# Batch 1 of a fused attention and feed-forward kernel: A@V in one burst behind FFN2, squares and a T copy on ScalarE, the first q cast by two engines

## The chip, the cores and the metric

The kernel runs on one core of a Trainium2 chip. A core has five engines with a queue each: TensorE (PE in the profile; its weight loads are PEld), VectorE (DVE), ScalarE (ACT), GpSimd (POOL) and SyncE (SP). Each works through its own queue in order, and they wait for one another through semaphores. The metric is the device time of one execution in microseconds.

## The reference

For 8 batches, 12 heads, 448 positions and a head dimension of 64, attention without softmax, and then a feed-forward layer with a PReLU:

```python
scores = scale * np.matmul(q, k.transpose(0, 1, 3, 2))      # scale = 1/sqrt(64)
attn = np.maximum(scores, 0.0) ** 2 / S                     # S = 448
attn_out = np.matmul(attn, v)
x = attn_out.transpose(0, 2, 1, 3).reshape(B * S, H * D)    # 3584 x 768
h = x @ w_in                                                # 768 x 2048
g = np.maximum(h, 0.0) + alpha * np.minimum(h, 0.0)
out = g @ w_out                                             # 2048 x 768
```

## The kernel before

**Quads and chunks.** Four heads of one batch make a quad; there are 3 quads a batch and 24 in all, numbered through. Positions are cut into 7 chunks (`j`) of 64. For a chunk, `score_mm` (L170) issues four matmuls of 64x64 weights and 448 columns, which run side by side in the four quarters of TensorE's array, into a pair of PSUM banks. `relu` (L181) moves the result to SBUF as bf16, on ScalarE ("A") or VectorE ("D"), and `square` (L189) squares it, on VectorE unless told otherwise. `sc` issues scores and relus and puts the chunks on the list `late`; `sq(k)` squares the first k of the list. `attnv` (L197) multiplies a quad's seven squared chunks by v (28 matmuls, accumulated in one pair of banks) and writes its halves to `xT`, one by ScalarE and one by VectorE.

**T.** Scores want q and k with the head dimension on the partitions. For the first quads `turn_pe` (L142) transposes on TensorE, 14 small matmuls for q and 14 for k, each set into one PSUM bank (or into more, by `cuts`), and copies the bank to `T` with VectorE or ScalarE. From quad 6 on `turn_dma` (L158) has VectorE rearrange and a DMA transpose.

**Feed-forward.** FFN1 unit `ff` of batch `b` (`f1`, L251) is six matmuls of 448 columns into one bank (`f1_mm`), and then `f1_out`: ScalarE computes neg = relu(-h), VectorE computes gT = neg * beta + h (L247, which frees the bank), and one chunk of `late` is squared, on VectorE. FFN2 (`f2`, L256) takes 128 positions and half of the output columns: 16 matmuls of 384 columns over all 16 units' gT, a copy by ScalarE, and two stores by SyncE. Two batches share a `gT`.

**Order.** No planner is at work: each engine's queue is the order in which the Python code issues, written out by hand for batches 0 and 1 (L277 to L377) and looped after that. PSUM's eight banks are handed out by `take_pair` and `take_bank`, the longest unused first, so an order on TensorE also sets which bank a group must wait for.

**Loads.** `load_qk`, `load_v`, `load_w_in` and `load_w_out` issue on POOL, in program order: q and k of a quad 224 KB each as they arrive in SBUF, v too, w_in in 16 pieces of 192 KB, w_out in two halves of 1536 KB. Every load uses one of eight semaphores in turn, so the issue of one waits until the load eight places earlier has landed. Quad 0's q and k come as fp32 by SyncE and ScalarE (`first`, L120) and are cast to bf16 at L130: q by VectorE whole, k by ScalarE in two pieces. All other loads cast on their way.

**The stretch around the change.** After `turn_pe(3)` (L347), batch 0's FFN1 units 4 to 15 alternate with scores of quads 3 and 4; FFN2 units of batch 0 follow, with A@V of quads 3 and 4 between them, the scores of quad 5, and then batch 1's FFN1, with A@V of quad 5 after its second unit.

Of the kernel before, what the change touches and what calls it, by code (L numbers as in the profile page):

```python
# [16 lines left out]
NJ = 7  # L17
# [3 lines left out]
def kernel(  # L21
# [10 lines left out]
    nc = tc.nc  # L32
    B, H, S, D = q.shape
# [3 lines left out]
    KM = d_model // 128  # L37
# [30 lines left out]
    def take(lo, n):  # L68
        clock[0] += 1
        for i in range(lo, lo + n):  # L70
            taken[i] = clock[0]

    def take_pair():
        lo = min((0, 2, 4, 6), key=lambda i: (max(taken[i], taken[i + 1]), i))
        take(lo, 2)
        return psum[:, lo:lo + 2]
# [7 lines left out]
    def take_bank():  # L84
        i = min(range(8), key=lambda i: (taken[i], i))
        take(i, 1)
        return psum[:, i]
# [4 lines left out]
    def load_qk(n):  # L92
        b, g = divmod(n, NG)
        for name, src in (("q", q), ("k", k)):
            t = raw_pool.tile([128, 2, NJ, D], BF16, tag=name, name=f"{name}raw")
            flat = src[b].rearrange("(m two) (pp j) d -> (two pp) m (j d)", two=2, j=NJ)
            nc.gpsimd.dma_start(out=t.rearrange("p m j d -> p m (j d)"), in_=flat[:, 2 * g:2 * g + 2])  # L97
            raw[(n, name)] = t

    def load_v(n):  # L100
        b, g = divmod(n, NG)
        t = v_pool.tile([128, 2, NJ, D], BF16, tag="v", name="vraw")
        flat = v[b].rearrange("(m two) (pp j) d -> (two pp) m (j d)", two=2, j=NJ)
        nc.gpsimd.dma_start(out=t.rearrange("p m j d -> p m (j d)"), in_=flat[:, 2 * g:2 * g + 2])  # L104
        vraw[n] = t
# [11 lines left out]
    def load_w_out(h):  # L117
        nc.gpsimd.dma_start(out=w_out_sb[:, h], in_=w_out_v[h])

    first = {}  # L120
# [6 lines left out]
    warm = psum[:, 7, :128]  # L127
    for _ in range(36):
        nc.tensor.matmul(warm, ident, ident, start=True, stop=True)
    for name, eng, cut in (("q", nc.vector.tensor_copy, ((0, NJ),)), ("k", nc.scalar.copy, ((0, 2), (2, NJ)))):  # L130
        t = raw_pool.tile([128, 2, NJ, D], BF16, tag=name, name=f"{name}raw")
        for lo, hi in cut:
            eng(t[:, :, lo:hi].rearrange("p m j d -> p m (j d)"), first[name][:, :, D * lo:D * hi])  # L133
        raw[(0, name)] = t
    for n in range(1, NG):
        load_qk(n)
# [5 lines left out]
    def turn_pe(n, cuts=((0, NJ, "D"),), cuts_k=((0, NJ, "D"),)):  # L142
        t = T_pool.tile([128, 2, NJ, 128], BF16, tag="T", name="T")
        for i, name in enumerate("qk"):
            src = raw.pop((n, name))
            for lo, hi, eng in (cuts, cuts_k)[i]:
                ps = take_bank().bitcast(BF16)
                for j in range(lo, hi):
                    for s in range(2):
                        nc.tensor.transpose(ps[64 * s:64 * s + 64, 128 * j:128 * j + 128], src[:, s, j], ident)  # L150
                dst = t[:, i, lo:hi].rearrange("p j c -> p (j c)")
                if eng == "D":
                    nc.vector.tensor_copy(dst, ps[:, 128 * lo:128 * hi])  # L153
                else:
                    nc.scalar.copy(dst, ps[:, 128 * lo:128 * hi])
        T[n] = t
# [13 lines left out]
    def score_mm(n, j):  # L170
        ps = take_pair()
        t = T[n]
        for r in range(2):
            for c in range(2):
                nc.tensor.matmul(ps[64 * c:64 * c + 64, r, :S],  # L175
                                 t[64 * r:64 * r + 64, 1, j, 64 * c:64 * c + 64],
                                 t[64 * r:64 * r + 64, 0, :, 64 * c:64 * c + 64],
                                 start=True, stop=True)
        return ps

    def relu(ps, eng):  # L181
        rl = rl_pool.tile([128, 2, S], BF16, tag="rl", name="rl")
        if eng == "A":
            nc.scalar.activation(rl, ps[:, :, :S], ACTF.Relu)  # L184
        else:
            nc.vector.tensor_scalar(rl, ps[:, :, :S], 0.0, None, ALU.max)  # L186
        return rl

    def square(n, j, rl, eng="D"):  # L189
        a = at_pool.tile([128, 2, S], BF16, tag="at", name="at")  # L190
        if eng == "A":
            nc.scalar.activation(a, rl, ACTF.Square)
        else:
            nc.vector.tensor_tensor(a, rl, rl, ALU.mult)  # L194
        att[(n, j)] = a

    def attnv(n):  # L197
        ps = take_pair()
        vv = vraw.pop(n)
        for j in range(NJ):  # L200
            a = att.pop((n, j))
            for r in range(2):
                for s in range(2):
                    nc.tensor.matmul(ps[64 * s:64 * s + 64, r, :S],  # L204
                                     vv[64 * r:64 * r + 64, s, j, :],
                                     a[64 * r:64 * r + 64, s],
                                     start=(j == 0), stop=(j == NJ - 1))
        b, g = divmod(n, NG)
        if g == 0:
            xT[b] = xT_pool.tile([128, NG, 2, S], BF16, tag="xT", name="xT")  # L210
        if n == 0:
            nc.scalar.activation(xT[b][:, g], ps[:, :, :S], ACTF.Copy, scale=out_scale)
            return
        nc.scalar.activation(xT[b][:, g, 0], ps[:, 0, :S], ACTF.Copy, scale=out_scale)  # L214
        nc.vector.tensor_scalar(xT[b][:, g, 1], ps[:, 1, :S], out_scale, None, ALU.mult)  # L215
# [3 lines left out]
    def sc(chunks):  # L219

        for n, j, eng in chunks:
            late.append((n, j, relu(score_mm(n, j), eng)))

    def sq(k=99):
        for g in late[:k]:
            square(*g)
        del late[:k]

    def run(chunks):
# [6 lines left out]
    def f1_mm(ps, b, ff, ks):  # L236
        for km in ks:
            nc.tensor.matmul(ps, w_in_sb[:, km // 2, km % 2, bass.ts(ff, 128)],  # L238
                             xT[b][:, km // 2, km % 2, :],
                             start=(km == 0), stop=(km == KM - 1))  # L240

    def f1_out(ps, b, ff):
        if b // 2 not in gT:
            gT[b // 2] = g_pool.tile([128, KF, 2 * S], BF16, tag="g", name="gT")
        neg = neg_pool.tile([128, S], F32, tag="neg", name="neg")
        nc.scalar.activation(neg, ps, ACTF.Relu, scale=-1.0)  # L246
        nc.vector.scalar_tensor_tensor(gT[b // 2][:, ff, (b % 2) * S:(b % 2) * S + S],  # L247
                                       neg, beta_sb[:, ff:ff + 1], ps, ALU.mult, ALU.add)
        sq(1)
# [6 lines left out]
    def f2(sb, c, hf, parts=((0, HALF),)):  # L256
        o = o_pool.tile([128, HALF], F32, tag="o", name="osb")
        for lo, hi in parts:
            ps = take_bank()[:, :hi - lo]
            for ff in range(KF):  # L260
                nc.tensor.matmul(ps, gT[sb][:, ff, bass.ts(c, 128)], w_out_sb[:, hf, ff, lo:hi],  # L261
                                 start=(ff == 0), stop=(ff == KF - 1))
            nc.scalar.copy(o[:, lo:hi], ps)  # L263
            for u in range(2):
                blk = 2 * c + u
                b, j = 2 * sb + blk // NJ, blk % NJ
                rows = out[b * S:(b + 1) * S].rearrange("(pp j) d -> j pp d", j=NJ)
                eng = nc.scalar if u and hi - lo < HALF else nc.sync
                eng.dma_start(out=rows[j][:, hf * HALF + lo:hf * HALF + hi], in_=o[64 * u:64 * u + 64, lo:hi])  # L269
# [4 lines left out]
    def ch(n, lo, hi, p=pat):  # L274
        return [(n, j, p[j]) for j in range(lo, hi)]

    load_w_in(0)  # L277
    load_w_in(1)
    turn_pe(0, ((0, 4, "D"), (4, NJ, "D")), ((0, 2, "A"), (2, NJ, "D")))
    sc(ch(0, 0, 4))  # L280
    sq(3)
    load_qk(3)
    load_v(3)
    sc(ch(0, 4, 6))
    turn_pe(1)
    sc(ch(0, 6, 7))
# [3 lines left out]
    sc(ch(1, 0, 3, "AAA"))  # L290
    attnv(0)
    load_qk(4)
    load_v(4)
    sq(2)
    sc(ch(1, 3, 4))
    turn_pe(2)
# [1 line left out]
    sc([(1, 4, "D"), (1, 5, "A"), (1, 6, "A")])  # L298
    sq(2)
    load_w_out(0)  # L300
    early = {}
    todo = []

# [8 lines left out]
    sq(3)  # L312
    attnv(1)
    load_qk(5)
    load_v(5)
    load_w_out(1)
    todo = [(ff, km) for ff in range(4) for km in range(4)]
# [15 lines left out]
    def f1s(b, lo, hi):  # L333
        for ff in range(lo, hi):
            f1(b, ff)
# [15 lines left out]
    sc(ch(3, 0, 3))  # L351
    f1s(0, 6, 8)
    sc(ch(3, 3, 6))
    f1s(0, 8, 10)
    turn_pe(4)
    load_qk(7)
    load_v(7)
    f1s(0, 10, 12)
    sc(ch(3, 6, 7) + ch(4, 0, 2))
    f1s(0, 12, 16)  # L360
    sc(ch(4, 2, 5))
    sq()
    f2(0, 0, 0)
    attnv(3)
    sc(ch(4, 5, 7))
    turn_pe(5)
    sq()
    load_qk(8)
    load_v(8)
    f2(0, 1, 0)  # L370
    sc(ch(5, 0, 2))
    attnv(4)
    sc(ch(5, 2, 4))
    sq()
    f2(0, 2, 0)
    sc(ch(5, 4, 7))
    sq()  # L377


    chunks = [(n, j) for n in range(2 * NG, NQ) for j in range(NJ)]  # L380
# [15 lines left out]
    for ff in range(4):  # L396
        ps = take_bank()[:, :S]
# [36 lines left out]
    for b in range(2, B):  # L434
# [15 lines left out]
        for i, u in enumerate(units):  # L450
            if i in at and not last:
                g = at[i]
# [37 lines left out]
```

## Time and profile before

| | us |
|---|---|
| median of 5 runs (lowest to highest) | 389.79 (389.72 to 390.11) |
| the profiled execution | 389.78 |
| its span in the profile | 388.0 |
| TensorE busy in the span | 378.8 |
| VectorE busy | 266.3 |
| ScalarE busy | 203.7 |

The span runs from the first to the last instruction of the trace; the 1.78 us between it and the profiled execution's time lie outside the trace. Times of a row are counted from the span's start. A busy engine's share doesn't say that it works at its peak: matmuls overlap, so the distance from one group's start to the next group's start says more than the sum of their lengths. An engine's idle time in the profile names the engine or load that ended last among those it waited for. The sections below use the page, the timeline, the chain of waits (what released each step, followed back from the end) and the loads' times from issue to landing.

### The profile page before, as it was taken

Reading aid. Unit: us, or ns where it says so; the run is one execution under the profiler, and the core shown is the slowest. Engines: PE = TensorE matmul, PEld = TensorE weight load, DVE = VectorE, ACT = ScalarE, POOL = GpSimd, SP = SyncE. Lnnn points to the kernel's source line nnn. Section 1 sums busy time; section 2 is a strip of 40 time slices with the busy share of each in tenths; the row PEclk is TensorE's granted clock in tenths of the full one; section 3 lists DMA queues with packets and bytes.
Section 4 is the critical chain, followed back from the end, with each engine's and each line's share of the span. In section 5 each row is a group of like instructions: output and inputs, shape, how many; then the busy total and the mean of one; then the engine's idle time right before and its main releaser. Section 6 shows DMA issues by size and latency. Waiting matters only on the chain.

```text
span 388.0 us, 7917 instructions
## 1 busy us (share of the span) xinstructions
PE 378.8 (98%) x3228; PEld 210.7 (54%) x3228; DVE 266.3 (69%) x422; ACT 203.7 (52%) x329; POOL 63.4 (16%) x94
## 2 busy tenths in 40 slices
PE   7799999999999999999999999999999999999996
PEld 5444454555665456644555455654555545655564
DVE  4977965776868878789755897689754887625300
ACT  5977656445545565466444664546543475434311
POOL 7458121422022102022010220120000000000000
PEclk9999999999999999999999999999999999999999
DMA  9999999899493774777292872937124300120023
GB/s 181 185 204 204 204 212 212 133 173 192 106 146 80 119 126 79 133 132 106 57 170 59 137 114 48 170 55 142 25 62 99 79 0 23 42 61 2 12 71 83
DMA packets 71093, 43.06 MB, mean 111 GB/s; under 512 B 38160, under 2 KB 71056, under 8 KB 71056
## 3 DMA queue, kind: packets, MB, share of 16 engines
q0 software_dynamic: 26496, 22.35, 39.6%
q1 hardware_dynamic: 44128, 19.65, 23.5%
q10 hardware_dynamic: 432, 0.56, 0.4%
q8 instruction: 25, 0.41, 0.4%
q14 instruction: 12, 0.10, 0.1%
HBM read 45.62 MB, written 11.01 MB: 146 GB/s over the span
## 4 chain that ended last, share of the span: by engine, by line
PE 90%; DVE 5%; ACT 2%; DMA 1%; issue 1%; ACTq 0%
PE psum L261 38%; PE psum L238 35%; PE psum L204 8%; PE psum L175 8%; DVE at L194 2%; ACT rl L184 2%; DMA qfirst<-in_q_dram 1%; DVE gT L247 1%; PE psum L150 1%; DVE T L153 1%; DVE rl L186 1%; ACT neg L246 0%; ACT osb L263 0%; DVE qraw L133 0%; ACTq L269 0%
## 5 line engine op out<-in xcount | busy, mean ns | idle before, releaser
L261 PE MATMUL psum<-w_out_sb,gT 128*128 128x384 bf16 (+2 forms) x912 | 151.1, 324 | 0.1
L238 PE MATMUL psum<-xT,w_in_sb 128*128 128x448 bf16 x768 | 149.5, 353 | 0.4 <-ACT rl L184 0.4
L261 PEld LDWEIGHTS <-gT 128*128 128x128 bf16 x912 | 86.5, 98 | 63.3 <-issue 8.6
L238 PEld LDWEIGHTS <-w_in_sb 128*128 128x128 bf16 x768 | 73.6, 98 | 72.5 <-issue 5.5
L246 ACT ACTIVATE neg<-psum 128x448 f32<-128x448 f32 x128 | 69.2, 546 | 66.3 <-PE psum L238 63.2
L247 DVE SCALAR_TENSOR_TENSOR gT<-neg,beta_sb,psum 128x448 bf16<-128x448 f32 x128 | 83.2, 676 | 29.5 <-ACT neg L246 29.5
L184 ACT ACTIVATE rl<-psum 128x896 bf16<-128x896 f32 x115 | 99.8, 937 | 0.5 <-PE psum L175 0.5
L194 DVE TENSOR_TENSOR at<-rl 128x896 bf16<-128x896 bf16 x167 | 93.8, 617 | 2.1 <-ACT rl L184 2.0
L186 DVE TENSOR_SCALAR rl<-psum 128x896 bf16<-128x896 f32 x53 | 57.5, 1086 | 40.8 <-PE psum L175 40.7
L263 ACT COPY osb<-psum 128x384 f32<-128x384 f32 (+2 forms) x57 | 27.0, 473 | 105.8 <-PE psum L261 101.1
L175 PE MATMUL psum<-T 64*64 64x448 bf16 x672 | 45.9, 356 | 2.4 <-ACT rl L184 0.9
L97 POOL DMA_DIRECT2D qraw<-in_q_dram x23 | 16.5, 719 | 178.0 <-DVE perm L161 166.9
L204 PE MATMUL psum<-at,vraw 64*64 64x448 bf16 x672 | 37.2, 351 | 0.6 <-ACT rl L184 0.2
L204 PEld LDWEIGHTS <-vraw 64*64 64x64 bf16 x672 | 23.9, 106 | 11.4 <-issue 3.2
L175 PEld LDWEIGHTS <-T 64*64 64x64 bf16 x672 | 18.1, 106 | 22.1 <-issue 15.6
L215 DVE TENSOR_SCALAR xT<-psum 128x448 bf16<-128x448 f32 x23 | 14.4, 624 | 16.0 <-PE psum L204 11.6
L97 POOL DMA_DIRECT2D kraw<-in_k_dram x23 | 16.7, 724 | 8.9 <-DMA w_out_sb<-in_moe_w_out_dram 5.4
L104 POOL DMA_DIRECT2D vraw<-in_v_dram x24 | 17.6, 732 | 0.7 <-issue 0.6
L214 ACT ACTIVATE xT<-psum 128x448 bf16<-128x448 f32 x23 | 12.7, 552 | 4.3 <-PE psum L204 4.3
L161 DVE COPY perm<-qraw 128x896 bf16<-128x896 bf16 x18 | 11.0, 612 | 4.2 <-DMA T<-perm 2.5
L114 POOL DMA_DIRECT2D w_in_sb<-in_moe_w_in_dram x16 | 10.0, 627 | 8.6 <-DMA kraw<-in_k_dram 3.2
L161 DVE COPY perm<-kraw 128x896 bf16<-128x896 bf16 x18 | 10.9, 608 | 0.0
(21 smaller groups left out, 35.8 us busy)
## 6 DMA issues: line engine op xcount, KB each, us to landing
out_dram<-osb SPq DMA_DIRECT2D x110, 96.0 KB, 2.2
vraw<-in_v_dram POOLq DMA_DIRECT2D x24, 224.0 KB, 7.2
qraw<-in_q_dram POOLq DMA_DIRECT2D x23, 224.0 KB, 4.7
kraw<-in_k_dram POOLq DMA_DIRECT2D x23, 224.0 KB, 6.7
w_in_sb<-in_moe_w_in_dram POOLq DMA_DIRECT2D x16, 192.0 KB, 8.8
w_out_sb<-in_moe_w_out_dram POOLq DMA_DIRECT2D x2, 1536.0 KB, 18.6
qfirst<-in_q_dram SPq DMA_DIRECT2D x1, 448.0 KB, 4.4
kfirst<-in_k_dram ACTq DMA_DIRECT2D x1, 448.0 KB, 4.7
```

Source lines behind the costliest of these rows:

```text
L97: nc.gpsimd.dma_start(out=t.rearrange("p m j d -> p m (j d)"), in_=flat[:, 2 * g:2 * g + 2])
L161: nc.vector.tensor_copy(p[:, i], raw.pop((n, name)).rearrange("p s j d -> p j s d"))
L175: nc.tensor.matmul(ps[64 * c:64 * c + 64, r, :S], t[64 * r:64 * r + 64, 1, j, 64 * c:64 * c + 64], t[64 * r:64 * r + 64, 0, :, 64 * c:64 * ...
L184: nc.scalar.activation(rl, ps[:, :, :S], ACTF.Relu)
L186: nc.vector.tensor_scalar(rl, ps[:, :, :S], 0.0, None, ALU.max)
L194: nc.vector.tensor_tensor(a, rl, rl, ALU.mult)
L204: nc.tensor.matmul(ps[64 * s:64 * s + 64, r, :S], vv[64 * r:64 * r + 64, s, j, :], a[64 * r:64 * r + 64, s], start=(j == 0), stop=(j == NJ ...
L238: nc.tensor.matmul(ps, w_in_sb[:, km // 2, km % 2, bass.ts(ff, 128)], xT[b][:, km // 2, km % 2, :], start=(km == 0), stop=(km == KM - 1))
L246: nc.scalar.activation(neg, ps, ACTF.Relu, scale=-1.0)
L247: nc.vector.scalar_tensor_tensor(gT[b // 2][:, ff, (b % 2) * S:(b % 2) * S + S], neg, beta_sb[:, ff:ff + 1], ps, ALU.mult, ALU.add)
L261: nc.tensor.matmul(ps, gT[sb][:, ff, bass.ts(c, 128)], w_out_sb[:, hf, ff, lo:hi], start=(ff == 0), stop=(ff == KF - 1))
L263: nc.scalar.copy(o[:, lo:hi], ps)
```

## The change

- Quad 0's q is cast in two pieces, chunks 0 to 3 by VectorE and 4 to 6 by ScalarE, ahead of ScalarE's casts of k. The copy of T for k's chunks 0 and 1, ScalarE's before, becomes VectorE's.
- The loads of v for quads 3 and 4 are issued later: quad 3's behind the first half of `w_out`, quad 4's behind q and k of quad 5.
- `turn_pe(4)` is issued after the matmuls of FFN1 unit 9 but ahead of that unit's `f1_out`, and its q copy goes to ScalarE.
- The three chunks 2 to 4 of quad 4 move from before the first FFN2 unit to behind it, and their squares behind A@V of quad 3; A@V of quad 3 then has three chunks before it and two after. Around A@V of quad 4 there are also three and two chunks in place of two and two, and the last FFN2 unit is followed by two chunks in place of three.
- The engines of the relus change: chunk 1 of quad 4 goes from VectorE to ScalarE, chunks 3 and 6 of quad 4 and 4 and 6 of quad 5 go to VectorE; chunk 1 of quad 5 stays there.
- `sq` takes an engine: two squares of quad 4 and three of quad 5 go to ScalarE.

```diff
-    for name, eng, cut in (("q", nc.vector.tensor_copy, ((0, NJ),)), ("k", nc.scalar.copy, ((0, 2), (2, NJ)))):
+    for name, cut in (("q", ((0, 4, nc.vector.tensor_copy), (4, NJ, nc.scalar.copy))),
+                      ("k", ((0, 2, nc.scalar.copy), (2, NJ, nc.scalar.copy)))):
         t = raw_pool.tile([128, 2, NJ, D], BF16, tag=name, name=f"{name}raw")
-        for lo, hi in cut:
-            eng(t[:, :, lo:hi].rearrange("p m j d -> p m (j d)"), first[name][:, :, D * lo:D * hi])
+        for lo, hi, copy in cut:
+            copy(t[:, :, lo:hi].rearrange("p m j d -> p m (j d)"), first[name][:, :, D * lo:D * hi])
...
-    def sq(k=99):
+    def sq(k=99, eng="D"):
         for g in late[:k]:
-            square(*g)
+            square(*g, eng)
         del late[:k]
...
-    turn_pe(0, ((0, 4, "D"), (4, NJ, "D")), ((0, 2, "A"), (2, NJ, "D")))
+    turn_pe(0, ((0, 4, "D"), (4, NJ, "D")), ((0, 2, "D"), (2, NJ, "D")))
     sc(ch(0, 0, 4))
     sq(3)
     load_qk(3)
-    load_v(3)
...
     load_qk(4)
-    load_v(4)
     sq(2)
...
     load_w_out(0)
+    load_v(3)
...
     load_qk(5)
+    load_v(4)
     load_v(5)
     load_w_out(1)
...
     sc(ch(3, 3, 6))
-    f1s(0, 8, 10)
-    turn_pe(4)
+    f1s(0, 8, 9)
+    ps = take_bank()[:, :S]
+    f1_mm(ps, 0, 9, range(KM))
+    turn_pe(4, ((0, NJ, "A"),))
+    f1_out(ps, 0, 9)
     load_qk(7)
     load_v(7)
     f1s(0, 10, 12)
-    sc(ch(3, 6, 7) + ch(4, 0, 2))
+    sc(ch(3, 6, 7) + ch(4, 0, 2, "AA"))
     f1s(0, 12, 16)
-    sc(ch(4, 2, 5))
-    sq()
     f2(0, 0, 0)
+    sc(ch(4, 2, 5, "AAADAAA"))
     attnv(3)
-    sc(ch(4, 5, 7))
+    sc(ch(4, 5, 7, "AAAAAAD"))
     turn_pe(5)
-    sq()
+    sq(3)
+    sq(2, "A")
     load_qk(8)
     load_v(8)
     f2(0, 1, 0)
-    sc(ch(5, 0, 2))
+    sc(ch(5, 0, 3))
     attnv(4)
-    sc(ch(5, 2, 4))
-    sq()
+    sc(ch(5, 3, 5, "AAAADAA"))
+    sq(3)
+    sq(2, "A")
     f2(0, 2, 0)
-    sc(ch(5, 4, 7))
-    sq()
+    sc(ch(5, 5, 7, "AAAAAAD"))
+    sq(1, "A")
+    sq(1)
```

## The prediction

> **What bounds the kernel now.** I read the page's first two parts, then TensorE's rows of the timeline in order of time, then the chain of waits for 28 to 66 us, then loads with their time to landing.
>
> ```profile
> PE 378.8 (98%) x3228; PEld 210.7 (54%) x3228; DVE 266.3 (69%) x422; ACT 203.7 (52%) x329; POOL 63.4 (16%) x94
> ...
> PE   7799999999999999999999999999999999999996
> PEld 5444454555665456644555455654555545655564
> DVE  4977965776868878789755897689754887625300
> ACT  5977656445545565466444664546543475434311
> ...
> PEclk9999999999999999999999999999999999999999
> DMA  9999999899493774777292872937124300120023
> ```
>
> TensorE is busy 98% at full clock, so only its remaining holes can be won; a hole shows as a group whose distance to the next start is longer than that of an equal group elsewhere. From 7.4 to 21.8 us VectorE and ScalarE are the limit instead (the 2 to 3 tenths missing in PE's first slices). DMA is full until about 66 us. After 84 us TensorE repeats one pattern and follows its own work, so what it gains before 66 us should reach the end one for one.
>
> ```profile
> 37.40 0.58 PE L150 MATMUL psum<-ident,qraw 128*64 128x128 bf16 x14
> 37.94 0.58 PE L150 MATMUL psum<-ident,kraw 128*64 128x128 bf16 x14
> 38.46 2.44 PE L238 MATMUL psum<-xT,w_in_sb 128*128 128x448 bf16 x12
> 40.83 1.08 PE L175 MATMUL psum<-T 64*64 64x448 bf16 x12
> ...
> 46.56 0.76 PE L175 MATMUL psum<-T 64*64 64x448 bf16 x12
> 47.44 2.76 PE L261 MATMUL psum<-w_out_sb,gT 128*128 128x384 bf16 x16
> ...
> 60.47 0.76 PE L175 MATMUL psum<-T 64*64 64x448 bf16 x12
> 61.16 1.69 PE L238 MATMUL psum<-xT,w_in_sb 128*128 128x448 bf16 x8
> 62.78 1.81 PE L204 MATMUL psum<-at,vraw 64*64 64x448 bf16 x28
> ```
>
> Columns: start, length, engine, line, operands, count. Four holes, each by start-to-start distance. Quad 4's transposes take 37.40 to 38.46 = 1.06 us, quad 3's 27.98 to 28.89 = 0.91: 0.15 lost, k having landed at 30.42 + 7.5 = 37.92. The 12 score matmuls at 40.83 take until 41.93 = 1.10, those at 60.47 take 0.69: 0.41 lost, to VectorE's second copy of quad 4's T (40.14 + 1.15 = 41.29). The 12 at 46.56 take 0.88: 0.19 lost, to VectorE's gT chain that releases the next PSUM bank (chain: gT ends 47.39). A@V of quad 5, 62.78 to 64.52 = 1.74 against 1.45 for the like burst at 341.22: 0.29 lost, to the last square (VectorE 63.53 + 0.62). Sum 0.15 + 0.41 + 0.19 + 0.29 = 1.04 us.
>
> **Start: q of quad 0 on two engines, one T copy from ScalarE to VectorE.** VectorE's cast of 896 columns takes 0.63 us at 5.13; 512 of them, by the copies of 512 and 384 (0.425 and 0.347 within the row of three), about 0.42: q's first transposes start 0.2 us earlier. ScalarE casts the other 384 from 5.13 to about 5.64 (its k casts of 256 and 640 columns, 0.41 and 0.72, give 0.51), so k's casts, which began at 5.44, come out some 0.10 late (6.58 instead of 6.47). VectorE then needs T of 512, 384 and now 256 columns before the first score: 6.06 + 0.34 + 0.26 + 0.28 = 6.94 (back-to-back copies overlap by 0.08), where the before had both engines done at 6.95. First scores at 7.0 either way. The last T piece comes 0.10 later, but feeds only chunk 2, whose relu stands in ScalarE's queue until 8.25 anyway. I take +0.02 us; ends −0.10 and +0.15, which pass undiminished because VectorE and ScalarE are the limit until 21.8.
>
> **Loads.** V of quads 3 and 4 go behind w_out's first half. POOL's issues wait for the load eight places back (those waits are in both programs), and the loads land in order of issue: k at 37.92, v at 31.14 + 7.9 = 39.04, w_out half at 32.05 + 14.7 = 46.75.
>
> ```profile
> kraw<-in_k_dram POOLq DMA_DIRECT2D x1, 224.0 KB, 7.5
> vraw<-in_v_dram POOLq DMA_DIRECT2D x1, 224.0 KB, 7.9
> w_out_sb<-in_moe_w_out_dram POOLq DMA_DIRECT2D x1, 1536.0 KB, 14.7
> ```
>
> One v is 1.12 us of queue, w_out 7.7. With one v fewer ahead, quad 4's k lands at 36.8 and the 0.15 hole goes. With two fewer w_out lands at 46.75 − 2.24 = 44.5. V of quad 3 follows at 45.6, q and k of quad 5 at 46.7 and 47.9, v of quad 4 at 49.0; from v of quad 5 on (34.95 + 15.2 = 50.15) the byte count is as before. POOL does change: k of quad 6 now waits for w_out (44.5 instead of being issued at 38.44), and everything behind it on POOL with it, but some 11 us of loads are outstanding then and k6 isn't used before 67 us. The Trainium skill's rule (DMA: Bandwidth & Descriptors, "Anatomy of one DMA — SWDGE (gpsimd) path") charges bytes over 436 GB/s, 0.53 us for one v: by it w_out would come only 1.05 us earlier, at 45.7. The row decides (204 GB/s here); both are ahead of the need below.
>
> **Quad 4's T.** q's copy goes to ScalarE, ahead of neg of unit 9, and VectorE's k copy ahead of that unit's gT. ScalarE's copy of 896 is not in the trace; 256 columns take 0.37, relu of 896 takes 0.92; I take 0.92, ends 0.75 and 1.1. It runs 38.0 to 38.9, k's on VectorE 39.0 to 39.6; the scores that want them come at 40.9. So 1.2 us of cover, and the 0.41 hole goes. Behind it, neg of unit 9 slips about a microsecond; its bank isn't asked for.
>
> **TensorE's new clock.** From 37.40, with distances from the rows: transposes 0.91 → 38.31; units 10, 11 2.37 → 40.68; scores 0.69 → 41.37; units 12–15 4.55 (24 matmuls before an FFN2 unit, at 135.91) → 45.92; FFN2 2.70 → 48.62; three chunks and A@V of quad 3; two chunks 0.48; transposes 0.91; FFN2 2.70; three chunks and A@V of quad 4; two chunks 0.51; FFN2 2.70; two chunks 0.50; 8 matmuls of batch 1 1.62; A@V of quad 5. A burst's three chunks take 0.60 at 100.06 and 0.68 at 206.94: the A@V pair contains the bank that ScalarE is just emptying of the FFN2 unit. I take 0.68, as both bursts stand behind single units, and 1.32 for A@V. That gives 50.62, 52.01, 54.71, 56.71, 59.92, 60.42, 62.04.
>
> Covers, need against supply: w_out 45.92 against 44.5. gT of unit 15 at 48.44: ScalarE's three relus (0.80 apart) from 41.17 let unit 12's neg start at 43.56, then VectorE alternates gT 0.59 and squares 0.54 from 44.15, ending unit 15 at 48.21: 0.2 to spare, and any lateness of VectorE beyond it stops TensorE in FFN2. V of quad 3 49.3 against 45.6.
>
> **Squares on ScalarE.** Five of quads 4 and 5, for which VectorE gets three more relus and sheds a T copy.
>
> ```profile
> 23.01 1.18 ACT L192 ACTIVATE at<-rl 128x896 bf16<-128x896 bf16 x1
> ...
> 63.53 0.62 DVE L194 TENSOR_TENSOR at<-rl 128x896 bf16<-128x896 bf16 x1 [0.18 <-ACT rl L184]
> ```
>
> The rule against it: the skill (ScalarE: Activation LUTs, "Rules for kernel authors") says multiplication and the like belong on VectorE; the rows agree on the price (1.18 against 0.62), but ScalarE is busy only 11.2 of 18 us from 48 to 66. Quad 4's two end at 54.6, wanted at 56.3. Quad 5's: relu of chunk 3 57.5 to 58.4, squares to 60.55 (the second half overlaps), then the waiting FFN2 copy (0.38, it was ready at 60.2; nobody asks for its bank yet), relu of chunk 5 60.92 to 61.84, its square to 63.02 plus hand-over 0.05 and the same-engine drain 0.05 = 63.12. A@V wants it at 62.04 + 5 × 0.19 = 62.99: 0.13 lost. By the same page's price ("What ACT_TABLE_LOAD costs": 186 ns and 0.833 per column, 0.93 for 896) nothing would be lost there; the row is the same operation and shape, so 1.18. So A@V takes 1.45 + 0.13, TensorE goes on at 63.62 instead of 64.52: **0.90 us gained**.
>
> Behind this, batch 1's third turn waits on VectorE for a transposing load that landed at 76.6; even if that doesn't move, unit 15's gT ends at 82.6 and FFN2, moved to 80.28, wants it at 82.8. Covered, barely.
>
> **Sum.** Profiled run 389.78 us (span 388.0, 1.78 outside it): 389.78 + 0.02 − 0.90 = 388.90. The median is 389.79, so the forecast is 0.23% less. About 0.2%, 0.78 us, is what a measurement of this kernel can tell from none: the threshold is 389.01.
>
> **Rivals.**
> - *The bursts and ScalarE eat it.* Both bursts wait 0.1 us longer for the FFN2 bank than at 206.94, quad 5's A@V keeps its old 0.29, the start costs 0.15: 0.90 − 0.2 − 0.16 − 0.13 = 0.41, 389.4; or less of this, 389.1. For: ScalarE's queue is in every one of these. Against: the clock above has them small.
> - *More than I count.* Bursts at 0.60, no wait in quad 5's A@V, start −0.10: 0.90 + 0.16 + 0.13 + 0.12 = 1.31, 388.5. For: both spellings of the burst are in the trace.
> - *A transfer after its new need (slower).* The first FFN2 unit now stands 1.5 us earlier and w_out's half must be there. Each us after 45.92 costs a us; at 46.8 the gain is gone, from 47.6 the kernel is slower by 0.2% (388.9 + 1.7 = 390.6), at 48 it takes 391.0. For: DMA is full, and this half took 14.7 us from its issue. Against: landing in order of issue puts it at 44.5, three us off.
> - *It changes nothing*: the holes move, as when the gT chain of unit 15 is 0.2 to 1 us late in FFN2: 389.1 to 389.8, counted with the first.
>
> **Chances.** Forecast 0.58 (own range 388.7 to 389.1), eaten 0.27, more 0.08, slower 0.07. Faster by over 0.2%: 0.54 of the forecast's and 0.08 = 0.62; within: 0.04 + 0.27 = 0.31; slower 0.07. Range 388.5 to 389.6: it reaches over the eaten case and the start's upper end, and leaves the late transfer out.
>
> **What will show it.** Right: quad 4's transposes at 0.91 with no gap before k; the scores behind unit 11 at 0.69; the first FFN2 near 45.9; A@V of quad 5 under 1.65; first scores at 7.0 ± 0.1; batch 1's unit 4 about 0.9 us earlier. Wrong: scores after 7.15; FFN2 waiting for a load or for VectorE's gT inside the first unit; bursts above 0.8; or the 88-matmul stretch of batch 1 broken by VectorE's wait.

## The result, and the profile after

The changed kernel takes 389.10 us (median of 22 runs); in the same sessions the kernel before took 389.92 (42 runs). The ratio is 0.9980, with a 95% interval of 0.9974 to 0.9986: 0.82 us or 0.2% faster, between 0.55 and 1.0 us by the interval. That is just about what can be told from no change. The profiled execution took 389.04 us, its span 387.3 us; before it was 389.78 and 388.0.

The page of the changed kernel, busy time and TensorE's row of the 40 slices:

```profile
PE 378.3 (98%) x3228; PEld 211.5 (55%) x3228; DVE 266.0 (69%) x420; ACT 206.4 (53%) x332; POOL 63.3 (16%) x94
...
PE   8799999999999999999999999999999999999996
```

ScalarE gained 2.7 us of work and VectorE lost 0.3. The page can't show more than that: TensorE is at 98% in both. The reading has to come from TensorE's rows in order of time. Line numbers are those of the changed kernel (about one above those of the kernel before: L151 transposes, L176 scores, L205 A@V, L239 FFN1, L262 FFN2).

TensorE's timeline of the changed kernel (start, length, engine, line, operation, operands, count):

```profile
37.47 0.58 PE L151 MATMUL psum<-ident,qraw 128*64 128x128 bf16 x14
37.89 0.56 PE L151 MATMUL psum<-ident,kraw 128*64 128x128 bf16 x14
38.38 2.44 PE L239 MATMUL psum<-xT,w_in_sb 128*128 128x448 bf16 x12
40.75 0.76 PE L176 MATMUL psum<-T 64*64 64x448 bf16 x12
41.47 4.70 PE L239 MATMUL psum<-xT,w_in_sb 128*128 128x448 bf16 x24
46.01 2.76 PE L262 MATMUL psum<-w_out_sb,gT 128*128 128x384 bf16 x16
48.70 0.76 PE L176 MATMUL psum<-T 64*64 64x448 bf16 x12
...
54.77 0.76 PE L176 MATMUL psum<-T 64*64 64x448 bf16 x12
55.41 1.52 PE L205 MATMUL psum<-at,vraw 64*64 64x448 bf16 x28
...
60.45 1.69 PE L239 MATMUL psum<-xT,w_in_sb 128*128 128x448 bf16 x8
62.06 1.52 PE L205 MATMUL psum<-at,vraw 64*64 64x448 bf16 x28
63.52 16.82 PE L239 MATMUL psum<-xT,w_in_sb 128*128 128x448 bf16 x88
80.17 1.14 PE L262 MATMUL psum<-w_out_sb,gT 128*128 128x384 bf16 x6
```

All four holes are gone. Quad 4's transposes take 37.47 to 38.38, 0.91 us instead of 1.06. The scores at 40.75 take 0.72 instead of 1.10. Nothing stands between 41.47 and the first FFN2 unit but 24 matmuls (4.54 us). A@V of quad 5 takes 62.06 to 63.52, 1.46 instead of 1.74. No row of this stretch carries an idle time.

From the start of quad 3's transposes (27.98 us before, 28.06 after) to the end of A@V of quad 5 (64.52 and 63.52) the stage took 36.54 us and now takes 35.46: 1.08 us gained. The lead is the same 1.01 us from 64 us on to TensorE's last matmul (384.22 before, 383.21 after), so what is gained before 66 us reaches TensorE's end undiminished. Then ScalarE's last copies and the last stores take 0.26 us back: from the start of that matmul to the end of the span it is 4.05 us in place of 3.79 (the last section shows where).

### The profile page after: what moved, and what is told of

Its sections match the earlier page's. It is cut to its first block, busy times and chain, and to the rows that moved or that the text cites. A ratio compares the mean times of both kernels' runs of the same rounds, so it can differ in the third digit from the quotient of the medians.

```text
span 387.3 us, 7916 instructions
## 1 busy us (share of the span) xinstructions
PE 378.3 (98%) x3228; PEld 211.5 (55%) x3228; DVE 266.0 (69%) x420; ACT 206.4 (53%) x332; POOL 63.3 (16%) x94
## 3 DMA queue, kind: packets, MB, share of 16 engines
HBM read 45.62 MB, written 11.01 MB: 146 GB/s over the span
## 4 chain that ended last, share of the span: by engine, by line
PE 94%; DVE 2%; ACT 1%; DMA 1%; issue 1%; ACTq 0%
PE psum L239 38%; PE psum L262 38%; PE psum L176 9%; PE psum L205 8%; ACT rl L185 1%; DMA qfirst<-in_q_dram 1%; PE psum L151 1%; DVE at L195 1%; DVE T L154 1%; DVE rl L187 0%; ACT osb L264 0%; ACTq L270 0%; DVE qraw L134 0%; ACT xT L215 0%; ACTq L264 0%
## 5 line engine op out<-in xcount | busy, mean ns | idle before, releaser
L262 PE MATMUL psum<-w_out_sb,gT 128*128 128x384 bf16 (+2 forms) x912 | 151.1, 324 | 0.0
L239 PE MATMUL psum<-xT,w_in_sb 128*128 128x448 bf16 x768 | 149.5, 353 | 0.4 <-ACT rl L185 0.4
L262 PEld LDWEIGHTS <-gT 128*128 128x128 bf16 x912 | 86.5, 98 | 63.1 <-issue 8.2
L239 PEld LDWEIGHTS <-w_in_sb 128*128 128x128 bf16 x768 | 73.6, 98 | 72.6 <-issue 5.7
L185 ACT ACTIVATE rl<-psum 128x896 bf16<-128x896 f32 x112 | 97.4, 937 | 1.1 <-PE psum L176 1.1
L195 DVE TENSOR_TENSOR at<-rl 128x896 bf16<-128x896 bf16 x162 | 90.7, 617 | 0.0
L187 DVE TENSOR_SCALAR rl<-psum 128x896 bf16<-128x896 f32 x56 | 60.8, 1086 | 42.1 <-PE psum L176 42.1
L176 PE MATMUL psum<-T 64*64 64x448 bf16 x672 | 45.7, 356 | 2.7 <-ACT rl L185 1.0
L205 PE MATMUL psum<-at,vraw 64*64 64x448 bf16 x672 | 37.0, 351 | 0.5 <-ACT rl L185 0.2
L176 PEld LDWEIGHTS <-T 64*64 64x64 bf16 x672 | 18.2, 106 | 21.9 <-issue 15.2
L205 PEld LDWEIGHTS <-vraw 64*64 64x64 bf16 x672 | 24.2, 106 | 10.8 <-issue 2.5
```

The source lines that it names most:

```text
L176: nc.tensor.matmul(ps[64 * c:64 * c + 64, r, :S], t[64 * r:64 * r + 64, 1, j, 64 * c:64 * c + 64], t[64 * r:64 * r + 64, 0, :, 64 * c:64 * ...
L205: nc.tensor.matmul(ps[64 * s:64 * s + 64, r, :S], vv[64 * r:64 * r + 64, s, j, :], a[64 * r:64 * r + 64, s], start=(j == 0), stop=(j == NJ ...
```

## The experiments

**Which part does the gain come from?** The forecast gave every part of the stage its own hole, 0.15 + 0.41 + 0.19 + 0.29, and the start nothing. Four kernels take one part each out of the changed kernel.

The loads put back where they were:

```diff
     load_qk(3)
+    load_v(3)
     ...
     load_qk(4)
+    load_v(4)
     ...
     load_w_out(0)
-    load_v(3)
     ...
     load_qk(5)
-    load_v(4)
```

> The changed kernel with the loads of v of quads 3 and 4 back in their old places. Theory (the loads have to move because the first FFN2 unit comes 1.4 us earlier): w_out's half lands 2.2 us later than the 43.9 of the changed kernel's profile, at 46.2 to 46.7, and FFN2, which starts at 46.0 there, waits for it 0.2 to 0.8 us; quad 4's k lands about 37.4, just in time. Loses 0.2 to 0.8 us of the 0.8 gained. Rival (the order of the loads is idle): no wait before FFN2, time as changed, about 389.1.

It took 389.44 us against 390.15 for the kernel before (ratio 0.9987, 0.9976 to 0.9998). Its timeline of TensorE has the wait with the load's name:

```profile
37.31 0.58 PE L151 MATMUL psum<-ident,qraw 128*64 128x128 bf16 x14
37.78 0.58 PE L151 MATMUL psum<-ident,kraw 128*64 128x128 bf16 x14
38.29 2.44 PE L239 MATMUL psum<-xT,w_in_sb 128*128 128x448 bf16 x12
...
46.55 1.15 PE L262 MATMUL psum<-w_out_sb,gT 128*128 128x384 bf16 x6 [0.47 <-DMA w_out_sb<-in_moe_w_out_dram]
```

The transposes of quad 4 are back at 0.98 us (37.31 to 38.29), and the 24 matmuls before FFN2 run from 41.36 to 46.55, 5.19 us instead of 4.54: 0.65 is the wait for w_out's half, which landed at 46.50. The stage takes 36.17 us, 0.71 of the 1.08 is lost. So FFN2 would have moved forward 0.65 us less without the two v moved back: w_out landed at 43.92 in the changed kernel, 2.6 us earlier than here, and at 43.57 to 45.04 in all profiles with the new order of loads. That is the rival "a transfer after its new need", made real by the old order of loads: 0.60 us after the need (46.50 against 41.36 + 4.54 = 45.90) cost 0.65. The median shows less of it than this one execution, which took 389.64: it is 0.38 us above the 389.06 of the kernel with the start undone, which ran in the same session and has the changed kernel's stage (below), and the fastest execution, at 389.11, lost next to nothing.

Both T copies of quad 4 on VectorE, at the new place:

```diff
-    turn_pe(4, ((0, NJ, "A"),))
+    turn_pe(4)
```

> The changed kernel with both copies of quad 4's T on VectorE, still issued ahead of unit 9's gT. Theory (what closes the 0.41 us hole before the scores of quad 4 is the place in VectorE's queue, but the 0.53 us of the copy then delays gT of units 9 and 10, which free unit 12's bank): scores of quad 4 keep 0.72 us, unit 12 waits about 0.5 us; 0.5 us slower than the changed kernel, 389.6. Rival A (the place alone is enough, the engine is free choice): as changed, 389.1. Rival B (the copy on ScalarE is what closes the hole): the scores take 1.1 us again.

389.57 us against 390.15 (ratio 0.9985, 0.9974 to 0.9995).

```profile
40.67 0.76 PE L176 MATMUL psum<-T 64*64 64x448 bf16 x12
41.92 4.70 PE L239 MATMUL psum<-xT,w_in_sb 128*128 128x448 bf16 x24 [0.49 <-DVE gT L248]
```

The scores' row is 0.76 us long, as in the changed kernel: T is there in time even from VectorE. But FFN1 unit 12, next in TensorE's queue, waits 0.49 us for a PSUM bank that VectorE's gT frees, and gT stands behind the copy. The stage takes 35.99 us, 0.53 is lost. So what ScalarE's copy buys is room in VectorE's queue, not an earlier T.

All squares on VectorE:

```diff
-    sq(3)
-    sq(2, "A")
+    sq()
     ...
-    sq(3)
-    sq(2, "A")
+    sq()
     ...
-    sq(1, "A")
-    sq(1)
+    sq()
```

> The changed kernel with all squares on VectorE. Theory (VectorE has got three more relus, the squares must go): the relu of quad 5's chunk 1 comes 0.8 us later on VectorE, the scores of chunk 4 of quad 5 wait about 0.5 us for its bank, and A@V of quad 5 ends a little later too; 0.5 us slower than the changed kernel, 389.6. Rival (the skill's price: ScalarE is the slower place, VectorE has room at 11 of 18 us): as changed or faster, 389.1 or less.

390.06 us against 390.15 (ratio 0.9994, 0.9986 to 1.0003).

```profile
57.02 0.39 PE L176 MATMUL psum<-T 64*64 64x448 bf16 x4
57.63 0.38 PE L176 MATMUL psum<-T 64*64 64x448 bf16 x4 [0.22 <-DVE rl L187]
57.95 2.77 PE L262 MATMUL psum<-w_out_sb,gT 128*128 128x384 bf16 x16
...
62.77 1.56 PE L205 MATMUL psum<-at,vraw 64*64 64x448 bf16 x28
64.26 2.06 PE L239 MATMUL psum<-xT,w_in_sb 128*128 128x448 bf16 x10
```

The two chunks of quad 5 before the last FFN2 unit take 0.93 us (57.02 to 57.95) instead of 0.51: the second waits for banks that a relu of VectorE is to free, and that relu stands behind VectorE's squares. A@V of quad 5 takes 1.49. The stage takes 35.91, 0.45 is lost. The loss stands at another place than the old hole, which was the last square before A@V. It is the price of the squares once VectorE has three more relus; the old engines of the relus were not tried with it.

The start undone (q of quad 0 cast by VectorE whole, k's first T copy on ScalarE, both lines as in the kernel before):

```diff
-    for name, cut in (("q", ((0, 4, nc.vector.tensor_copy), (4, NJ, nc.scalar.copy))),
-                      ("k", ((0, 2, nc.scalar.copy), (2, NJ, nc.scalar.copy)))):
+    for name, eng, cut in (("q", nc.vector.tensor_copy, ((0, NJ),)), ("k", nc.scalar.copy, ((0, 2), (2, NJ)))):
...
-    turn_pe(0, ((0, 4, "D"), (4, NJ, "D")), ((0, 2, "D"), (2, NJ, "D")))
+    turn_pe(0, ((0, 4, "D"), (4, NJ, "D")), ((0, 2, "A"), (2, NJ, "D")))
```

> The changed kernel with the start as before (q cast by VectorE alone, first k part of T by ScalarE). Theory (the three copies of T that the first scores want take as long on VectorE alone as before on two engines): 0 within 0.1 us, 389.1. Rival A (the start gains some 0.2 us, hidden in the one profile by a TensorE that came to full clock 1.7 us later): 389.3. Rival B (the start costs 0.1 us): 389.0.

389.06 us against 390.15 (ratio 0.9976, 0.9968 to 0.9985), and the changed kernel had 389.10 in its own session. Quad 3's transposes began 22.88 us behind the landing of quad 0's q, in the changed kernel's second profile (below) 22.90: the new start is worth nothing. The stage takes 35.46 us like the changed kernel's.

**Built up from the other side.** The kernel before, with the moved loads alone; the changed kernel ran beside it a second time.

> The changed kernel once more, on the chip of the next three. Theory (the slow first transposes in its first profile are TensorE's clock, whose release comes at another moment in each execution, and no effect of the change): transposes of quad 0 at 28 to 30 ns each and first scores 1.9 us after quad 0's q has landed, not 2.1. Rival (casting q earlier itself meets the slow clock): slow again. Time 0.8 us under the kernel before.

> The kernel before with only the loads of v of quads 3 and 4 moved. Theory: quad 4's k lands 1.1 us earlier and its transposes take 0.91 us instead of 1.06, but the scores behind unit 11 still wait for VectorE's second copy of T, which hangs on VectorE's own queue, so they come no earlier: 0, within 0.05 us at batch 1's unit 4. Rival (each hole counts on its own, as the sum of the prediction had it): 0.15 us faster.

The changed kernel took 389.23 against 390.09 (ratio 0.9979, 0.9969 to 0.9990), its stage again 35.46. The loads alone took 390.00 (ratio 0.9997, 0.9988 to 1.0006). Their timeline:

```profile
37.95 0.58 PE L150 MATMUL psum<-ident,qraw 128*64 128x128 bf16 x14
38.37 0.56 PE L150 MATMUL psum<-ident,kraw 128*64 128x128 bf16 x14
38.86 2.44 PE L238 MATMUL psum<-xT,w_in_sb 128*128 128x448 bf16 x12
41.23 0.38 PE L175 MATMUL psum<-T 64*64 64x448 bf16 x4
41.90 0.57 PE L175 MATMUL psum<-T 64*64 64x448 bf16 x8 [0.28 <-DVE T L153]
42.49 4.70 PE L238 MATMUL psum<-xT,w_in_sb 128*128 128x448 bf16 x24
```

The hole in the transposes is closed (0.91 us) and comes out again behind it: the scores take 41.23 to 42.49, 1.26 us instead of 1.10, because TensorE is earlier and VectorE's T copy is not. The stage is 36.54 us, not a hundredth less than before.

Loads, and quad 4's transposes moved with q's copy on ScalarE (the stretch from FFN2 on left as it was):

```diff
-    f1s(0, 8, 10)
-    turn_pe(4)
+    f1s(0, 8, 9)
+    ps = take_bank()[:, :S]
+    f1_mm(ps, 0, 9, range(KM))
+    turn_pe(4, ((0, NJ, "A"),))
+    f1_out(ps, 0, 9)
```

> The kernel before with the loads moved and quad 4's T as in the change (issued ahead of unit 9's outputs, q's copy on ScalarE), everything else old. Theory: the scores behind unit 11 take 0.70 us instead of 1.10, together with k's 0.15 some 0.5 us; but the gT chain that releases the bank of the first FFN2 unit is VectorE's own (it ended at 47.4 in the profile before), so part of it may be lost there again: 0.2 to 0.55 us faster, and a longer wait before FFN2. Rival (the holes before 44 us add up): 0.55 us faster with the old 0.19 before FFN2.

389.50 us against 390.09 (ratio 0.9993, 0.9983 to 1.0004: three of its twelve executions took 390.6 to 391.4, and the interval doesn't tell it from no change). Its stage is surer: 36.01 us, 0.53 gained. The scores at 40.88 take 0.72. The scores ahead of FFN2 still take 0.87 (46.23 to 47.10): this hole of 0.19 stays until the chunks are moved behind FFN2.

Together, each kernel's stage from quad 3's transposes to the end of A@V of quad 5:

| kernel | stage, us | gained |
|---|---|---|
| before | 36.54 | |
| loads alone | 36.54 | 0.00 |
| loads, and T of quad 4 | 36.01 | 0.53 |
| these and the new order around FFN2, squares on VectorE | 35.91 | 0.63 |
| the whole change | 35.46 | 1.08 |
| the whole but the loads | 36.17 | 0.37 |
| the whole but ScalarE's T copy | 35.99 | 0.55 |

Taken out one at a time, loads, T copy and squares cost 0.71 + 0.53 + 0.45 = 1.69 us, and yet the whole gains 1.08. The parts are links of one chain: each is worth what it is worth only when the others are there. The new order around FFN2 and the new engines of the relus were not run apart from each other; together, with the squares still on VectorE, they bring 0.10 (third and fourth row).

**Can the start be won after all?** The first score of the changed kernel comes 2.13 us behind q's landing in its first profile and 1.92 in its second; before it was 1.90. Two theories: ScalarE's free time can take q's second T copy from VectorE, or it is k's casts that hold it.

```diff
-    turn_pe(0, ((0, 4, "D"), (4, NJ, "D")), ((0, 2, "D"), (2, NJ, "D")))
+    turn_pe(0, ((0, 4, "D"), (4, NJ, "A")), ((0, 2, "D"), (2, NJ, "D")))
```

> The changed kernel with the copy of T for q's chunks 4 to 6 of quad 0 on ScalarE. Theory (the first scores wait for three copies in a row on VectorE, while ScalarE is idle from 6.4 to 7.5 us): the first scores come about 0.1 us earlier, not more, since the transposes of k's second part stand before them on TensorE; all of it reaches the end, 0.1 us under the changed kernel. Rival (the first scores wait for TensorE anyway): 0.

389.16 us against 390.09 (ratio 0.9979, 0.9971 to 0.9988): no better than the changed kernel. TensorE's timeline of it:

```profile
5.74 0.58 PE L151 MATMUL psum<-ident,qraw 128*64 128x128 bf16 x14 [0.36 <-DVE qraw L134]
6.15 0.28 PE L151 MATMUL psum<-ident,kraw 128*64 128x128 bf16 x4
6.75 0.47 PE L151 MATMUL psum<-ident,kraw 128*64 128x128 bf16 x10 [0.32 <-ACT kraw L134]
7.15 1.04 PE L176 MATMUL psum<-T 64*64 64x448 bf16 x12
```

The first score follows directly on k's second transposes, and those wait for ScalarE's cast of k. VectorE's T copies were not the limit; the theory was wrong and the rival right. So, with the edit above, k's chunks 2 to 6 cast by VectorE:

```diff
-                      ("k", ((0, 2, nc.scalar.copy), (2, NJ, nc.scalar.copy)))):
+                      ("k", ((0, 2, nc.scalar.copy), (2, NJ, nc.vector.tensor_copy)))):
```

> The changed kernel with the cast of k's chunks 2 to 6 of quad 0 on VectorE, and q's second T copy on ScalarE. Theory (the first scores stand behind the transposes of k's second part, and those behind ScalarE's third cast, which the change made 0.1 us later; moving one T copy alone therefore gave nothing): with the cast on VectorE at 5.5 to 6.0 the transposes run through, and the first scores come 1.7 us after q's landing instead of 1.92; since VectorE and ScalarE are the limit until 21.8 us, 0.2 us less at batch 1 and at the end, some 1.0 us under the kernel before. Rival (something else, such as VectorE's chain of T copies, sets the first scores): 1.9 us again, time as changed.

389.34 us against 389.94 (ratio 0.9989, 0.9979 to 0.9999). The first score comes 1.66 us behind q's landing instead of 1.92, as foretold. But its further timeline reads

```profile
6.98 0.98 PE L176 MATMUL psum<-T 64*64 64x448 bf16 x16 [0.18 <-ACT T L156]
8.38 0.75 PE L176 MATMUL psum<-T 64*64 64x448 bf16 x8 [0.42 <-ACT rl L185]
9.50 0.58 PE L151 MATMUL psum<-ident,qraw 128*64 128x128 bf16 x14 [0.37 <-DMA qraw<-in_q_dram]
10.58 0.58 PE L151 MATMUL psum<-ident,kraw 128*64 128x128 bf16 x14 [0.50 <-DMA kraw<-in_k_dram]
```

and quad 1's transposes wait for their loads, which landed at 9.46 and 10.54 in this execution. The quarter of a microsecond is spent there. The same kernel again, to see whether that is a rule:

> The same kernel as with k's cast split, once more. In its first profile the first scores came 0.27 us earlier behind q's landing, and the gain was gone by 28 us, while quad 1's k landed at 10.5 us and its transposes stood waiting for it. Theory (the next limit of the start is the landing of quad 1's q and k, which differs between executions): where they land at 8.5 and 9.6 us as in the changed kernel's profile, quad 3's transposes start about 22.7 us behind q's landing, against 22.9 to 23.1; on the average over executions 0 to 0.2 us under the changed kernel. Rival (the 0.27 us are lost in the chain of relus and squares whatever the loads do): 22.9 or later also with early loads.

388.92 us against 390.00 (ratio 0.9974, 0.9963 to 0.9985). Here quad 1's loads landed at 8.61 and 9.70, and quad 3's transposes began 22.66 us behind q's landing; 22.90 in the changed kernel's second profile. So the start is worth a quarter of a microsecond where the loads are early. Over the two sessions this version is 0.60 and 1.08 us faster than the kernel before, the changed kernel 0.82 and 0.86: nothing shows that it beats it.

**The case where stage and time differ.** The kernel with all squares on VectorE gained 0.63 us in the stage and 0.09 in its median. It ran once more.

> The same kernel as with all squares on VectorE, once more, since its median (0.09 us under the kernel before) and its profile (from quad 3's transposes to batch 1 0.63 us less than before) differ by more than the other runs' do. Theory (the rest is where early loads land in an execution): the stage again 35.9 us, and a median some 0.5 us under the kernel before, 389.5. Rival (squares on VectorE cost something elsewhere that the stage doesn't show): a median again within 0.2 us of the kernel before.

389.88 us against 390.00 (ratio 1.0003, 0.9989 to 1.0017): the rival came true. The stage is again 35.92 us, 0.62 less than before, so the reading of the stage holds. The rest of its profile is later at both ends: quad 3's transposes began 0.34 us later than before, and from TensorE's last matmul to the end of the span it took 4.44 us (4.32 in its first profile) in place of 3.79. So the sum comes out: 0.34 − 0.62 + 0.65 = 0.37, by which its span of 388.39 exceeds the 388.01 of before. The start's part is scatter (quad 0's q landed 0.12 later, and TensorE began at half rate); the end's part came in both profiles. The last two stores landed 2.4 and 2.7 us behind their issue, those of the kernel before 1.8 and 2.1. Why this kernel's last stores should land later wasn't found; its program after 66 us is that of the changed kernel. It stays open, and the value of the squares, 0.45 us, is shown for the stage and not for the whole.

## Why the prediction was right or wrong, point by point

- **TensorE's holes are what can be won, and the lead passes on.** Right: the lead of 1.01 us stays from 64 us to TensorE's last matmul, and the FFN2 unit at 80.17 follows an unbroken run of 88 FFN1 matmuls. The cover called bare held: VectorE's third turn moved along, the transposing load that it waits for landing at 75.24 instead of 76.52.
- **Four holes that add up.** Right as a sum for the whole change, wrong if read one by one: the 0.15 of the transposes is worth 0.00 with the loads alone, because TensorE then meets VectorE's T copy sooner. What the prediction had wrong here is the pairing of each hole with its own cure.
- **Loads.** Right in order and nearly in size: w_out's half was forecast at 44.5 and landed at 43.92, v of quad 3 at 45.6 and 45.08, q of quad 5 at 46.7 and 46.19, v of quad 4 at 49.0 and 48.50. The trace's 1.12 us for one such load holds (45.08 to 46.19, 46.19 to 47.32), and with the old order w_out lands 2.6 us later, by two v. So the row of the trace (2.24 us for two) was nearer than the 1.05 us worked out from the Trainium skill's 436 GB/s. But that working took the 224 KB of a v as they arrive. The profile of either kernel counts 45.62 MB read from HBM, which is all the inputs as fp32, so a v is 448 KB read. By these bytes the same rule gives an estimate of 1.05 us for one v and 2.1 for two, close to the row; which bytes a casting load is charged for, the rule doesn't say.
- **T copy on ScalarE: 0.92 us, 38.0 to 38.9.** It took 0.91 us from 38.10. The stall was to go with the copy; it would have gone with VectorE too, only to come back at unit 12's bank, which the forecast did not name.
- **The clock from 37.40 on.** Right to a few hundredths: FFN2 was put at 45.92 and 48.62 and came at 46.01 and 48.70, with everything 0.08 later from the start on. Too dear by 0.08 was the term of the two bursts: three chunks ahead of A@V took 0.64 and 0.64, not 0.68.
- **Squares on ScalarE at 1.18.** This term was mis-sized, by 0.13 us of the result. ScalarE's timeline of the changed kernel:

```profile
20.70 2.75 ACT L185 ACTIVATE rl<-psum 128x896 bf16<-128x896 f32 x3
23.09 1.18 ACT L193 ACTIVATE at<-rl 128x896 bf16<-128x896 bf16 x1
...
58.34 1.79 ACT L193 ACTIVATE at<-rl 128x896 bf16<-128x896 bf16 x2
60.05 0.48 ACT L264 COPY osb<-psum 128x384 f32<-128x384 f32 x1
60.42 0.92 ACT L185 ACTIVATE rl<-psum 128x896 bf16<-128x896 f32 x1
61.38 0.95 ACT L193 ACTIVATE at<-rl 128x896 bf16<-128x896 bf16 x1
```

 The square at 61.38 takes 0.95 us; of two in a row, 1.79 together, the second starts 0.86 behind the first. The square at 23.09, from which the price came, still shows 1.18; but the relus ahead of it end at 20.70 + 2.75 = 23.45, so 0.36 of its length lies beside them and only 0.82 behind. The last square was done at 62.33 (61.38 + 0.95), ahead of its need at 62.99, and A@V lost nothing. The figure of the Trainium skill that the forecast set aside (ScalarE: Activation LUTs, "What ACT_TABLE_LOAD costs", 0.93 for 896 columns, with an overlap of 0.09 back to back) is what the runs show. Its rule that such work belongs on VectorE ("Rules for kernel authors") would have been the wrong guide for these five squares: VectorE's 0.62 is cheaper, but VectorE is the queue that TensorE waits for, and with the relus placed as in the change, keeping the squares there loses 0.45 us of the stage.
- **Start +0.02.** Quad 3's transposes began 0.08 later, and undoing the start changed nothing. Right that it is worth nothing, and right in part for the reason: what sets the first score is k's way through ScalarE and TensorE, where the forecast had VectorE's three T copies.
- **The sum.** 0.90 was forecast for the stage and 1.08 came: 0.13 for the square and 0.08 for the bursts, less some hundredths in the scores. Of that the end of the kernel took 0.26 back, for which the sum had no term (a pause of ScalarE, last section), and the start 0.06 more than its 0.02: 389.78 + 0.08 − 1.08 + 0.26 = 389.04, the profiled execution. So the forecast of 388.90 is 0.14 below it, where the missing end alone would have made it 0.26: that the mis-sized square and bursts took back part of that is luck. Between the medians 0.82 us was gained, of a forecast 0.88, and the median of 389.10 stands at the edge of the forecast's own range, 388.7 to 389.1.
- **The rivals.** "The bursts and ScalarE eat it" did not happen: no burst was above 0.64. "More than I count" was right in its mechanism (bursts, no wait in A@V: 1.08 against its 1.31) but did not show in the time. The late transfer did not come, and the run with the old order of loads shows that the danger was real.

## What to carry to other kernels

When TensorE waits in several places of one stage, don't price the holes one at a time: ask what the same engine meets next once it is earlier, and move loads, copies and bank releases together. Take an instruction's price from distances between starts or from one that stands alone, since the length of a queued one contains its wait beside the one before. Give work to the engine whose queue nobody waits for, even where it takes half as long again.

## What the runs showed of the hardware that was not expected

**TensorE begins some executions at half its rate, for longer.** In three of the thirteen profiles (the changed kernel's, the loads alone, the second of the squares on VectorE) quad 0's transposes ran at about half rate. Here are the changed kernel's first rows, and then those of its second profile:

```profile
5.45 0.96 PE L151 MATMUL psum<-ident,qraw 128*64 128x128 bf16 x14
6.20 0.78 PE L151 MATMUL psum<-ident,kraw 128*64 128x128 bf16 x14
7.08 1.07 PE L176 MATMUL psum<-T 64*64 64x448 bf16 x16
```

```profile
5.55 0.58 PE L151 MATMUL psum<-ident,qraw 128*64 128x128 bf16 x14 [0.70 <-DVE qraw L134]
5.97 0.28 PE L151 MATMUL psum<-ident,kraw 128*64 128x128 bf16 x4
6.57 0.47 PE L151 MATMUL psum<-ident,kraw 128*64 128x128 bf16 x10 [0.32 <-ACT kraw L134]
6.97 1.23 PE L176 MATMUL psum<-T 64*64 64x448 bf16 x16
```

The 14 transposes of q take 0.75 us from start to start in the one and 0.42 in the other. From q's landing to the first score it is 2.1 to 2.3 us in the three and 1.90 to 1.93 in the others with the same or the old start, so it costs 0.2 to 0.4 us. The page's clock row, in tenths of 10 us slices, doesn't show it, but the trace's own record of the granted clock does: full clock begins at 6.61, 6.88 and 7.20 us in the three, and at 4.05 to 5.92 in the other ten (4.98 before, 4.14 in the changed kernel's second profile). So it is the granted clock, and a scatter of executions rather than an effect of the change: the changed kernel shows both. This fits what the Trainium skill says (TensorE: Matmul & The Clock Gate, "Part 1: The HAM clock gate"), that the clock is released by a window of some 3.4 us which runs freely and doesn't start with the kernel; that the release follows such a window was not tested here.

**ScalarE pauses some 0.28 us at one place of its program, and where that falls decides the end.** From TensorE's last matmul to the end of the span it took 3.77 to 3.88 us in the kernel before, the loads alone, the loads with T, and the start with q's second T copy on ScalarE; 4.05 to 4.13 in the seven other profiles of the changed order; and 4.3 to 4.4 in the two of the squares on VectorE. The three groups don't overlap, so this goes with the kernel and is not scatter. ScalarE's last three copies, before and after:

```profile
382.18 0.48 ACT L263 COPY osb<-psum 128x384 f32<-128x384 f32 x1 [2.42 <-PE psum L261]
383.63 0.37 ACT L263 COPY osb<-psum 128x256 f32<-128x256 f32 x1 [0.97 <-PE psum L261]
...
384.63 0.27 ACT L263 COPY osb<-psum 128x128 f32<-128x128 f32 x1 [0.62 <-PE psum L261]
```

```profile
380.87 0.48 ACT L264 COPY osb<-psum 128x384 f32<-128x384 f32 x1 [2.12 <-PE psum L262]
382.90 0.37 ACT L264 COPY osb<-psum 128x256 f32<-128x256 f32 x1 [1.55 <-PE psum L262]
...
383.90 0.27 ACT L264 COPY osb<-psum 128x128 f32<-128x128 f32 x1 [0.63 <-PE psum L262]
```

A copy that waits for TensorE usually starts 0.04 us after its wait ended. The copy at 382.18 in the kernel before and the one at 382.90 in the changed kernel start 0.33 and 0.32 after it, and both are the 576th instruction that the trace records on ScalarE, semaphore waits counted. In eleven of the thirteen profiles the 576th is late by as much. The changed kernel has three instructions fewer (584 in place of 587), so the pause moves from a copy that held nothing up to the next one, and the last copy and the last store stand behind that. The last copy starts 0.68 us behind the start of TensorE's last matmul in place of 0.40, and that is the 0.26 which the end took back. With q's second T copy on ScalarE the 576th is itself a wait, and the end takes 3.79 again; but there the 320th, 256 earlier, is a copy, it is late too, and TensorE waits for it and comes to its last matmul 0.28 later. What the pause is stays open, and so do the two profiles of the squares on VectorE: they show no such pause at the 576th (the wait ahead of the last store), and their last stores land late. Differences of about 0.3 us at the start and at the end are a third of what this change was worth, so a single total should be split into start, stage and end before it is explained.
